# A fused attention and expert kernel: its hand-planned step list replaced by a second one

## The chip, the cores and the metric

The kernel runs on one core of one Trainium2 chip. Five engines work side by side, each through its own queue in order: PE (matrix products into PSUM), ACT (activations and copies), DVE (vector work and copies), POOL (masks, and the issue of the input loads) and SP (the issue of output stores and of crossbar transposes). The metric is device time of one execution in microseconds (us); lower is better. PSUM has eight banks, numbered 0 to 7.

## The reference

Two layers run one after the other over 8 batches of 576 tokens. The first is attention with 8 heads of 64, whose keys and values are averaged over 8 neighbouring tokens; the second is a causal attention in four experts, of which each token takes the best two. Cut to what matters:

```python
k_p = k.reshape(B, H, Sp, pool, D).mean(axis=3)      # pool = 8, Sp = 72
v_p = v.reshape(B, H, Sp, pool, D).mean(axis=3)
attn = softmax(scale * q @ k_p.T)                    # written out in the reference
x = (attn @ v_p) as [B, S, H * D]
logits = x @ w_gate; the best 2 of 4 experts, softmax over the two -> w
for e in range(4):
    a = softmax(causal(scale * (x @ wq[e]) @ (x @ wk[e]).T))
    out += w[e] * (a @ (x @ wv[e])) @ wo[e]
```

## The kernel before

The work of each batch is cut into small steps. A step belongs to one engine. The order of all steps on all engines is one text, `SEQ` (lines 622 to 694), which a planner's search wrote out; the loop behind it (line 696) reads it word by word and records each step's instructions, and each engine runs its own steps in that order. Waits between engines follow from which tile a step reads or writes. So the text alone decides what stands behind what on each engine, which PSUM bank a PE step writes, and on which of two engines a copy runs.

A word is name, arguments, a colon and the batch: `E1:4@26` is step E, argument 1, batch 4, in the banks from 2 and from 6 on. `@` gives the PSUM bank or banks of a PE step; a `d` at the end puts a copy on DVE, without it the copy runs on ACT; a `p` leaves the output store to a later word; a `c` runs a dummy matmul on 32 output rows only.

The steps in the order in which a batch passes through them:

- `L_k`, `L_q`, `L_v` (line 112): loads of the input, issued by POOL, which convert to bf16 on the way. `W` loads weights. For batch 0, `R` and `Q` load parts unconverted on other queues; `r` (line 140) and `w` (line 147) convert them, `c` orders weights.
- `PK`, `kc`, `kt` (lines 264 to 281): pool the keys on PE, transpose on DVE, copy to `kpT`. `PV`, `vc` (283, 286): the same for the values.
- `u` (line 292): DVE transposes q into `qT`. `u0` needs the pieces `L_q0` and `L_q2`, `u1` needs `L_q1` and `L_q3`.
- `E` (line 309): scores, in four banks; `e` (line 319): exp on ACT, each call over two banks. `E2` is the narrow one for the last 64 tokens.
- `D`, `d`, `x` (337 to 353): softmax denominators by PE, then logarithm and exp on ACT. `O`, `o` (356, 364): attention output on PE, scaled on DVE into `xT`.
- `V`, `v` (381, 391) and `P`, `p` (449, 457): projections of the experts, and their copies out of PSUM. `p_t` is the copy for the last 64 tokens. `g0` to `g9` (396): the gate.
- `S`, `s`, `a` (467, 480, 498): expert scores, exp on ACT, causal mask on POOL. Three of four `s` steps cover 128x1024.
- `B`, then `bz`, `bg`, `b` (526, 539): expert outputs on PE, and their scaling on DVE into `osc`.
- `osc` is transposed into `oT` on PE with a copy (`T`, `t`, lines 559 and 564) for batches 0, 1, 6 and 7, and by a crossbar DMA from SP's queue (`F`, line 574) for batches 2 to 5. `F10:5` moves the main part of expert pair 1 of batch 5, `F11:5` its tail.
- `Y`, `y`, `zs` (582, 592, 607): output projection on PE, copy to `ofin`, output store on SP's queue.
- `H` (line 205): dummy matmuls on a constant tile; nobody reads them.

Raw inputs have three buffers, so a load of batch b+3 waits for the steps that read batch b. PSUM banks have no fixed owner: a PE step that takes a bank waits for the bank's last reader.

Of the kernel before, what the change touches and what calls it, by code (L numbers as in the profile page):

```python
# [21 lines left out]
def kernel(  # L22
# [584 lines left out]
    def z(b, c, queue):  # L607
# [20 lines left out]
        d2:0 H1:0@1 H1:0@1 o10:0 x2:0 H1:0@1 H1:0@1 o20:0 H1:0@1 W3:0 H1:0@0 o11:0 H1:0@0 H1:0@0 c2:0d P_q0:0@2 L_v0:1
        c3:0d P_k0:0@3 L_v1:1 p_q0:0 P_t0:0@5 L_v2:1 p_k0:0 PK:1@2 p_t0:0 S00:0@0 L_k0:2 kc:1 S01:0@4 S02:0@6 s00:0
        P_q1:0@3 L_k1:2 kt:1d s02:0 L_k2:2 P_k1:0@2 u1:1 s01:0 a00:0 u0:1 a02:0 E1:1@06 p_k1:0 p_q1:0d L_q0:2 e11:1  # L630
        c4:0d L_q1:2 E0:1@24 e10:1 L_q2:2 V0:0@6 V1:0@7 e00:1 L_q3:2 v0:0d V2:0@0 v1:0d a01:0 V3:0@6 e01:1 v2:0d L_v0:2
        S12:0@2 v3:0d s12:0 g1:0 E2:1@04 L_v1:2 PV:1@6 g2:0 e21:1 g3:0 D0:1@7 e20:1 D1:1@2 a12:0 vc:1d H1:0@3 d0:1
# [10 lines left out]
        L_v2:4 g8:1 P_k0:2@3 g9:1 bz12:0 e00:3 bg12:0 L_k0:5 b12:0 PV:3@2 p_k0:2d L_k1:5 e01:3 E1:3@04 vc:3d B12:1@3
        L_k2:5 e10:3 P_k1:2@6 bz12:1 L_q0:5 bg12:1 b12:1 e11:3 T11:0@2 B02:0@7 p_k1:2d L_q1:5 V3:2@3 t11:0 bz02:0
        D0:3@0 a00:1 bg02:0 v3:2 O20:2@6 b02:0 D2:2@2 PK:4@1 d0:3 u0:4 L_q2:5 O00:3@3 O11:3@7 x0:3 a11:1 kc:4 D1:3@0
        T00:0@4 d2:2 V1:2@5 L_q3:5 d1:3 o00:3 T02:0@2 V0:2@1 x2:2 a10:1 t00:0d t02:0 Y3:0@0 x1:3 o20:2 L_v0:5 v0:2d
        S00:2@2 y3:0p O01:3@6 o11:3 D2:3@1 PV:4@4 s00:2 L_v1:5 zs3:0 o01:3 O10:3@0 B01:1@7 vc:4d d2:3 kt:4 Y1:0@6
# [5 lines left out]
        x0:4 S10:2@2 L_v1:6 p_t0:3d S12:2@6 O10:4@5 s10:2 p_k0:3d PV:5@0 a02:2 o10:4 O01:4@1 O00:4@4 vc:5 L_v2:6 D2:4@2
        V2:3@3 o01:4 d2:4 s12:2 B10:1@0 a10:2 o00:4 V3:3@2 B11:1@1 bz10:1 L_k0:7 v2:3 bg10:1 E2:5@46 v3:3 b10:1 V4:3@3
        bz11:1 e20:5 L_k1:7 bg11:1 b11:1 e21:5 V0:4@0 v4:3 g4:2 S03:2@4 L_k2:7 x2:4 S01:3@6 v0:4d S01:2@2 s03:2 T11:1@1
        g1:3 s01:3 T01:1@0 L_q0:7 T10:1@4 P_k0:4@5 t11:1d t10:1d t01:1d s01:2 g2:3 L_q1:7 Y3:1@4 g3:3 p_k0:4d E0:5@06
# [6 lines left out]
        B11:2@1 s12:3 p_k0:5d F00:2 a00:3 E0:6@26 bz11:2 bg11:2 P_q0:5@0 x2:5 b11:2 a12:3 e00:6 u1:6 F11:2 B00:3@1
        e01:6 p_q0:5d E1:6@24 bz00:3 F10:2 B11:3@0 bg00:3 b00:3 e10:6 V1:5@6 bz11:3 Y0:1@1 bg11:3 F01:3 e11:6 v1:5d
        B01:3@7 b11:3 Y2:1@6 y0:1p bz01:3 D0:6@0 bg01:3 b01:3 y2:1p PK:7@4 zs0:1 g1:4 O20:5@1 d0:6 D1:6@7 zs2:1 kc:7
        S12:4@2 F00:3 d1:6 P_k1:5@6 o20:5 s12:4 kt:7d g2:4 Y3:2@7 p_k1:5d x1:6 S03:4@0 S00:5@2 a12:4 S10:4@4 y3:2dp
        s03:4 V2:5@6 s00:5 a03:4 g3:4 V4:5@0 zs3:2 g4:4 v2:5d B10:3@7 s10:4 v4:5d a00:5 P_t0:5@6 bz10:3 E2:6@02 bg10:3
        x0:6 O01:6@4 a10:4 p_t0:5d e20:6 PV:7@5 b10:3 e21:6 O11:6@6 o01:6 O00:6@0 vc:7 F11:3 D2:6@7 O10:6@1 S01:4@2
# [107 lines left out]
```

## Time and profile before

| | us |
|---|---|
| median of 3 runs (156.7, 157.54, 157.59) | 157.54 |
| the profiled execution | 157.23 |
| its span, first to last instruction | 155.5 |
| busy: PE, ACT, DVE, POOL | 145.2, 137.8, 124.2, 89.0 |

The span is what the trace shows; 1.73 us of the execution's own time lie around it. Busy time is the time in which at least one instruction of the engine is under way; matmuls overlap, so PE's figure is no measure of how far PE is from its limit. PE's granted clock is 0.99 of full speed over the span. Line 220 is the helper of all matrix products, and line 211 that of all copies, so rows are told apart by the tiles they name. "From A to B" times count from the start of the span. In rows of single instructions the bracket at the end gives the engine's idle time ahead of it and what ended it.

### The profile page before, as it was taken

What the parts mean: (1) busy time and instruction counts of PE and PEld (TensorE: products, weight loads), DVE (VectorE), ACT (ScalarE), POOL (GpSimd) and SP (SyncE); (2) the same over time, 40 slices, a digit from 0 to 9 for tenths busy, and PEclk for the clock granted to TensorE, in tenths of its full rate; (3) what the DMA queues carried; (4) which work ended last, traced back from release to release, by engine and by line L of the source; (5) the groups of instructions that cost most, each with busy time, mean ns of one, the idle gap of its engine ahead of it and who ended that gap; (6) DMA issues with size and microseconds to landing.
All of it is one profiled execution on the core that took longest, in us unless ns stands there. A gap on an engine that the chain in (4) does not pass through costs nothing.

```text
span 155.5 us, 5467 instructions
## 1 busy us (share of the span) xinstructions
PE 145.2 (93%) x2131; PEld 79.1 (51%) x2131; DVE 124.2 (80%) x407; ACT 137.8 (89%) x255; POOL 89.0 (57%) x160
## 2 busy tenths in 40 slices
PE   6998998999999999999999999999999999969980
PEld 2332452454664365455736556475465765526640
DVE  1862826889889889989898999999988888957860
ACT  3369579999999999999999999999999999969970
POOL 6996488999689988855999141224100434323200
PEclk9999999999999999999999999999999999999997
DMA  4999999999999999999999963431480552387894
GB/s 121 239 187 184 177 179 180 180 180 190 180 179 180 182 177 181 213 251 178 180 180 213 181 75 76 146 104 34 126 279 8 108 173 72 82 198 267 282 377 161
DMA packets 68746, 26.67 MB, mean 171 GB/s; under 512 B 62704, under 2 KB 63728, under 8 KB 68720
## 3 DMA queue, kind: packets, MB, share of 16 engines
q0 software_dynamic: 57264, 14.72, 95.0%
q1 hardware_dynamic: 11088, 10.88, 22.8%
q10 hardware_dynamic: 368, 0.72, 1.5%
q8 instruction: 16, 0.26, 0.7%
q14 instruction: 10, 0.08, 0.2%
HBM read 30.42 MB, written 9.44 MB: 256 GB/s over the span
## 4 chain that ended last, share of the span: by engine, by line
PE 54%; DMA 19%; POOL 9%; ACT 7%; DVE 4%; issue 4%; POOLq 0%; SPq 0%; DVEq 0%; ACTq 0%
PE psum L220 53%; DMA qraw<-in_q_dram 11%; DMA wst_q<-in_moe_wq_dram 5%; DMA oT<-osc 3%; POOL kraw L125 3%; POOL qraw L125 3%; ACT eta L330 3%; ACT etb L493 2%; POOL vraw L125 1%; POOL etb L510 1%; PE psum L229 1%; DVE qT L297 1%; ACT rza L353 1%; ACT rza L349 1%; DVE osc L552 1%
## 5 line engine op out<-in xcount | busy, mean ns | idle before, releaser
L493 ACT ACTIVATE etb<-psum 128x1024 bf16<-128x1024 f32 x48 | 47.2, 1029 | 0.7 <-PE psum L220 0.4
L510 POOL TENSOR_SCALAR_AFFINE_SELECT etb<-etb 128x256 bf16<-128x256 bf16 x64 | 25.9, 416 | 30.0 <-ACT etb L493 29.1
L330 ACT ACTIVATE eta<-psum 96x1024 bf16<-96x1024 f32 (+1 forms) x48 | 36.0, 807 | 0.6 <-PE psum L220 0.2
L220 PEld LDWEIGHTS <-etb 128*128 128x128 bf16 x480 | 18.6, 97 | 7.9 <-issue 2.8
L376 DVE TENSOR_TENSOR xT<-psum,rza 128x512 bf16<-128x512 f32 x32 | 20.5, 681 | 2.1 <-ACT rza L353 2.0
L220 PE MATMUL psum<-wop,oT 128*128 128x512 bf16 (+1 forms) x74 | 20.4, 373 | 1.7 <-DMA oT<-osc 1.4
L125 POOL DMA_DIRECT2D qraw<-in_q_dram x29 | 19.1, 661 | 4.3 <-DMA vraw<-in_v_dram 2.9
L220 PE MATMUL psum<-vaug,etb 128*128 128x65 bf16 x480 | 21.2, 193 | 0.2 <-POOL etb L510 0.2
L125 POOL DMA_DIRECT2D kraw<-in_k_dram x25 | 19.0, 765 | 3.0 <-issue 0.9
L125 POOL DMA_DIRECT2D vraw<-in_v_dram x24 | 18.5, 774 | 3.7 <-PE psum L220 2.9
L220 PE MATMUL psum<-wvg,xT 128*128 128x260 bf16 x144 | 20.5, 274 | 0.0
L220 PE MATMUL psum<-xT,wqp 128*128 128x64 bf16 (+1 forms) x128 | 19.6, 286 | 0.0
L220 PE MATMUL psum<-xT,wkp 128*128 128x512 bf16 (+1 forms) x128 | 19.5, 286 | 0.0
L552 DVE TENSOR_TENSOR osc<-psum,gt 128x256 bf16<-128x256 f32 (+2 forms) x40 | 16.6, 422 | 1.0
L220 PE MATMUL psum<-qk 64*128 64x64 bf16 (+4 forms) x192 | 16.1, 277 | 0.2
L220 PEld LDWEIGHTS <-xT 128*128 128x128 bf16 x144 | 12.7, 97 | 6.3 <-issue 2.5
L211 ACT COPY ofin<-psum 128x512 f32<-128x512 f32 (+1 forms) x25 | 13.9, 581 | 2.1 <-PE psum L220 1.8
L211 DVE CAST qk<-psum 128x512 bf16<-128x512 f32 (+1 forms) x24 | 14.6, 615 | 1.3 <-PE psum L220 0.6
L297 DVE STREAM_TRANSPOSE qT<-qraw 128x576 f32<-128x576 f32 (+1 forms) x17 | 13.2, 789 | 2.9 <-DMA qraw<-in_q_dram 2.2
L220 PE MATMUL psum<-qT,kpT 32*128 32x64 bf16 (+1 forms) x256 | 13.3, 289 | 1.6 <-ACT eta L330 0.6
L208 PE MATMUL psum<-warm 128*128 128x512 bf16 x41 | 12.8, 461 | 1.3 <-DVE onesd L176 1.3
L220 PE MATMUL psum<-eta,vp 96*32 96x512 bf16 (+1 forms) x256 | 13.1, 288 | 0.2 <-DVE vp L211 0.2
(78 smaller groups left out, 215.8 us busy)
## 6 DMA issues: line engine op xcount, KB each, us to landing
out_dram<-ofin SPq DMA_DIRECT2D x32, 256.0 KB, 2.6
vraw<-in_v_dram POOLq DMA_DIRECT2D x24, 192.0 KB, 6.8
kraw<-in_k_dram POOLq DMA_DIRECT2D x21, 192.0 KB, 7.5
qraw<-in_q_dram POOLq DMA_DIRECT2D x28, 144.0 KB, 7.8
out_dram<-ofin SPq DMA_DIRECT2D x7, 128.0 KB, 2.5
xT<-in_q_dram ACTq DMA_DIRECT2D x2, 288.0 KB, 4.7
xT<-in_k_dram SPq DMA_DIRECT2D x2, 192.0 KB, 5.0
kraw<-in_k_dram POOLq DMA_DIRECT2D x4, 96.0 KB, 5.2
```

Of the source, the lines that this page charges most:

```text
L125: nc.gpsimd.dma_start(out=dst, in_=src)
L208: nc.tensor.matmul(out=psum[rows, bank, :], lhsT=warm[:, rows], rhs=warm[:], start=True, stop=True)
L211: (nc.vector.tensor_copy if dve else nc.scalar.copy)(out=out, in_=in_)
L220: nc.tensor.matmul(out=out, lhsT=lhsT, rhs=rhs, start=start, stop=stop)
L229: nc.tensor.transpose(out=out[s], in_=in_[:, s], identity=ident[0:n, 0:n])
L297: nc.vector.transpose(out=dst.rearrange("p (a s n) -> p a n s", s=32, n=n)[:, :, own], in_=src.rearrange("p (a n d) -> p a n d", n=n, d=32 ...
L330: nc.scalar.activation(out=dst, in_=src, func=EXP, scale=ATT_EXP_SCALE)
L349: nc.scalar.activation(out=rz, in_=z, func=LN)
L376: nc.vector.tensor_tensor(out=xT[:, 2 * got[0][0] + t : 2 * got[-1][0] + t + 1 : 2, m + got[0][1].start : m + got[0][1].stop], in0=psum[:, ...
L493: nc.scalar.activation(out=et[:, ep, :, eo : eo + n], in_=psum[:, bank : bank + 2, 0:n], func=EXP, scale=MOE_EXP_SCALE,)
L510: nc.gpsimd.affine_select(out=blk, in_=blk, pattern=[[0, 2], [1, 128]], compare_op=ISGE, fill=0.0, base=0, channel_multiplier=-1,)
L552: nc.vector.tensor_tensor(out=osc(b, ep)[:, own, :].rearrange("p c (e d) -> p e c d", e=2), in0=o[:, :, :, 0:HD], in1=gt.to_broadcast([128 ...
```

## The change

The text `SEQ` is replaced by another that holds the same steps of the computation, each with the same arguments. No function changes. There are three kinds of difference.

The order of the steps, almost everywhere behind the first line, and the banks of most PE steps. The loads keep their order among themselves.

The engine of some copies. Counted over the text, on ACT before and after (the rest runs on DVE):

| copy | on ACT before | on ACT after |
|---|---|---|
| `y` (to `ofin`, whole) | 24 | 18 |
| `p` (512 columns) | 14 | 15 |
| `p_t` | 2 | 4 |
| `vc` | 2 | 4 |
| `v` (two copies each) | 14 | 13 |
| `kt` | 6 | 4 |
| `t` (256 columns / 64 columns) | 3 / 3 | 4 / 5 |
| `r` | 1 | 0 |

The number of dummy matmuls: 41 before, 43 after, three of which use 32 output rows.

The diff at the places that the prediction speaks of:

```diff
-        R0:0 R1:0 Q0:0 Q1:0 I:0 H14:0@0 L_k20:0 L_k01:0 L_k11:0 J:0 K:0 M:0 L_k21:0 L_q1:0 w0:0 L_v0:0 r0:0d w1:0 u00:0
-        L_v1:0 r1:0 N:0 L_v2:0 PK0:0@0 H1:0@1 W0:0 H1:0@1 H1:0@1 u01:0 H1:0@1 W1:0 kc0:0 PK1:0@1 kt0:0 L_k0:1 kc1:0
...
-        v1:1 S12:1@6 s02:1 u0:3 S03:1@4 B11:0@3 a01:1 L_q2:4 u1:3 P_q0:2@2 s03:1 s12:1 bz11:0 a03:1 bg11:0 S11:1@0 g1:1
...
-        b02:1 e00:4 u1:4 P_q1:3@7 L_k1:6 y2:0dp e01:4 E1:4@02 L_k2:6 p_q1:3d V0:3@6 zs2:0 e10:4 L_q0:6 g1:2 T12:0@4
-        P_t0:2@7 v0:3d P_k1:3@5 L_q1:6 e11:4 t12:0d p_t0:2d g2:2 u1:5 V1:3@4 p_k1:3 L_q2:6 T02:1@2 E2:4@06 v1:3 D0:4@3
...
-        a12:2 y3:1p g4:3 V1:4@2 g5:2 u0:6 L_q2:7 e01:5 zs3:1 P_k1:4@3 v1:4d L_q3:7 g0:3 g6:2 e00:5 E1:5@46 g5:3 a01:2
...
-        F00:5 g2:7 Y0:2@7 s02:6 bz10:5 a10:6 B11:5@0 bg10:5 b10:5 P_k0:7@1 s11:6 bz11:5 a02:6 bg11:5 b11:5 F11:5
-        B00:6@6 y0:2dp Y3:4@2 p_k0:7 a11:6 Y1:4@0 bz00:6 y3:4p zs0:2 bg00:6 F10:5 B11:6@1 b00:6 y1:4p S02:7@4 zs3:4
-        bz11:6 S01:7@2 g0:7 bg11:6 S00:7@6 zs1:4 s02:7 b11:6 P_q1:7@0 g3:7 g4:7 g5:7 s00:7 g6:7 B10:6@1 a02:7 T00:6@4
-        P_k1:7@5 bz10:6 bg10:6 p_q1:7 t00:6d a00:7 b10:6 s01:7 T11:6@4 Y1:5@6 p_k1:7d Y3:5@7 t11:6d y1:5p S03:6@0 a01:7
...
+        R0:0 R1:0 Q0:0 Q1:0 I:0 H14:0@0 L_k20:0 L_k01:0 L_k11:0 J:0 K:0 M:0 L_k21:0 L_q1:0 w0:0 L_v0:0 r0:0d w1:0 r1:0d
+        L_v1:0 u01:0 L_v2:0 u00:0 PK0:0@0 H1:0@1 W0:0 H1:0@1 kc0:0 H1:0@1 H1:0@1 kt0:0d W1:0 N:0 PK1:0@0 E0:0@24 L_k0:1
...
+        E2:0@02 E1:0@46 e21:0 H1:0@4c e20:0 H1:0@4c L_q1:1 e11:0 H1:0@4c e10:0 PV:0@0 L_q2:1 D0:0@1 D2:0@6 vc:0d d0:0
...
+        V4:1@1 V1:1@6 p_q1:1d L_q1:4 v4:1 T10:0@0 S03:1@2 u0:3 v1:1 a01:1 S11:1@4 s03:1 L_q2:4 S02:1@6 u1:3 s11:1
...
+        e00:4 t02:0d t00:0d P_k0:3@1 v1:3d L_k1:6 e01:4 g1:2 E2:4@26 B12:1@0 p_k0:3d L_k2:6 e21:4 S02:2@4 e20:4 bz12:1
+        T01:1@1 bg12:1 E1:4@26 s02:2 b12:1 t01:1d g2:2 B10:1@0 L_q0:6 g3:2 V0:3@1 e11:4 bz10:1 B02:1@4 bg10:1 L_q1:6
+        v0:3d P_k1:3@5 e10:4 bz02:1 bg02:1 a02:2 b10:1 B11:1@1 b02:1 p_k1:3 u1:5 T12:1@0 L_q2:6 S10:2@6 t12:1 S11:2@2
...
+        E2:5@02 g6:2 T11:1@4 L_k2:7 p_t0:3d Y1:0@5 e21:5 t11:1d e20:5 S03:2@6 S01:2@2 L_q0:7 y1:0dp S12:2@0 s03:2
...
+        e11:5 u1:6 P_k0:4@5 a01:2 y3:1dp e10:5 L_q3:7 E0:5@26 p_k0:4d zs3:1 L_v0:7 PV:5@4 e00:5 g2:3 D2:4@5 V1:4@0 g3:3
...
+        bz11:5 a00:6 bg11:5 b11:5 B10:6@7 bg10:5 S00:7@0 p_q1:7 b10:5 a12:6 S02:6@2 V0:7@4 s00:7 bz10:6 F11:5 bg10:6
+        b10:6 Y2:4@6 v0:7d s02:6 Y0:4@5 a00:7 y2:4dp Y3:4@7 F10:5 S02:7@0 y0:4p zs2:4 a02:6 y3:4dp S01:7@2 V1:7@6 s02:7
+        zs0:4 zs3:4 B00:6@7 P_k1:7@5 v1:7d s01:7 a02:7 g1:7 Y0:3@6 bz00:6 bg00:6 g0:7 p_k1:7 b00:6 Y1:4@4 a01:7 g2:7
+        y0:3p Y1:3@2 g3:7 g4:7 S12:7@0 y1:4p zs0:3 g5:7 S03:6@6 y1:3dp T00:6@5 s12:7 T10:6@3 zs1:4 Y3:5@4 t00:6d zs1:3
...
```

More of the change, by code (lines that the diff above doesn't have):

```diff
@@ L628 @@
[L628 to L632, printed above, removed]
@@ L643 @@
[L643 to L647, printed above, removed]
@@ L653 @@
[L653 to L656, printed above, removed]
-        a12:2 y3:1p g4:3 V1:4@2 g5:2 u0:6 L_q2:7 e01:5 zs3:1 P_k1:4@3 v1:4d L_q3:7 g0:3 g6:2 e00:5 E1:5@46 g5:3 a01:2
@@ L663 @@
[L663 to L667, printed above, removed]
```

98 lines of the change are left out of this document (57 added, 41 removed).

## The prediction

> **What bounds the kernel now.** I read the page first, then the engines' busy time by stretch, then the waits of the transposes that follow the loads, then the tail. The page's head, and its picture of the DMA engines in 40 slices:
>
> ```profile
> span 155.5 us, 5467 instructions
> PE 145.2 (93%) x2131; PEld 79.1 (51%) x2131; DVE 124.2 (80%) x407; ACT 137.8 (89%) x255; POOL 89.0 (57%) x160
> DMA  4999999999999999999999963431480552387894
> ```
>
> PE shows most, but a matmul's record overlaps the next one (a dummy's row further down shows it), so 93% isn't PE at its limit. The DMA engines are full from the second slice to about slice 22, some 86 us: that is the stream of q, k and v. By stretch (columns: length, then busy time and count of PE, PEld, DVE, ACT, POOL, then clock, DMA share, GB/s):
>
> ```profile
> 47.00:136.00 89.00, 88.42 (x1390) 50.76 (x1389) 81.50 (x270) 87.75 (x166) 46.97 (x91) 1.00 1.06 148
> 136.00:140.00 4.00, 2.58 (x21) 0.97 (x20) 2.20 (x6) 2.71 (x7) 0.95 (x3) 1.00 0.82 198
> ```
>
> From 47 to 136 us ACT works 87.75 of 89.00 us: there ACT is the bound, and DVE has 7.50 us of idle time. Before 47 us something else sets the pace. The DVE rows of the q transposes (start, length, engine, and in brackets what DVE waited for) say what:
>
> ```profile
> 23.85 1.44 DVE L297 STREAM_TRANSPOSE qT<-qraw 128x576 f32<-128x576 f32 x2 [0.93 <-DMA qraw<-in_q_dram]
> 35.32 1.44 DVE L297 STREAM_TRANSPOSE qT<-qraw 128x576 f32<-128x576 f32 x2 [0.18 <-DMA qraw<-in_q_dram]
> 46.46 1.44 DVE L297 STREAM_TRANSPOSE qT<-qraw 128x576 f32<-128x576 f32 x2 [0.36 <-DMA qraw<-in_q_dram]
> 66.91 0.78 DVE L297 STREAM_TRANSPOSE qT<-qraw 128x576 f32<-128x576 f32 x1 [0.47 <-DMA qraw<-in_q_dram]
> ```
>
> By their order in the list these are batches 1, 2, 3 and 5, some 11 us apart from batch to batch, each started when its q had just landed. POOL's loads stand in the same order in both lists and the DMA engines are full, so these landings stay where they are. Work taken from an engine ahead of such a row buys waiting at that row and no time at the end. I therefore take the start of `u0:3` at 46.46 as a clock, and count only what changes behind it. The last piece is the tail (PE, then ACT, then SP's queue, then the chain that ended last):
>
> ```profile
> 138.48 0.82 PE L220 MATMUL psum<-wop,oT 128*128 128x512 bf16 x3 [1.42 <-DMA oT<-osc]
> 138.91 0.59 ACT L211 COPY ofin<-psum 128x512 f32<-128x512 f32 x1 [1.29 <-PE psum L220]
> 134.62 0.53 SPq L615 DMA_DIRECT2D out_dram<-ofin  x1
> 135.21 1.25 SPq L580 DMA_TRANSPOSE oT<-osc  x1
> 135.21 3.23 DMA oT<-osc
> ```
>
> Crossbar step `F10:5` was issued at 135.21, right behind the output store `zs0:2` (134.62), and landed 3.23 us later. PE stood 1.42 us at `Y1:5` for it, ACT 1.29 us behind PE.
>
> **The change part by part.** The sum is made against the profiled execution, 157.23 us (span 155.5 and 1.73 around it); it lies 0.31 below the median of 157.54, within the three runs.
>
> *Copies that change engine.* ACT's prices, by form:
>
> ```profile
> L211 ACT COPY ofin<-psum 128x512 f32<-128x512 f32 x24 | 13.6, 589 | 1.6 <-PE psum L220 1.3
> L211 ACT CAST qk<-psum 128x512 bf16<-128x512 f32 x14 | 8.3, 590 | 2.9 <-PE psum L220 2.9
> L211 ACT CAST qk<-psum 128x256 bf16<-128x256 f32 x2 | 0.8, 382 | 0.0
> L211 ACT CAST vp<-psum 96x512 bf16<-96x512 f32 x2 | 1.2, 582 | 0.0
> L211 ACT CAST vaug<-psum 128x256 bf16<-128x256 f32 x14 | 5.2, 383 | 0.0
> L211 ACT COPY L<-psum 128x4 f32<-128x4 f32 x14 | 2.5, 182 | 0.0
> L211 ACT COPY oT<-psum 128x64 bf16<-128x64 bf16 x3 | 0.6, 229 | 0.0
> L211 ACT COPY oT<-psum 128x256 bf16<-128x256 bf16 x3 | 1.1, 371 | 0.4 <-PE psum L229 0.4
> L211 ACT CAST kpT<-kf 128x192 bf16<-128x192 f32 x2 | 0.7, 352 | 1.2 <-DVE kf L277 1.2
> L211 ACT CAST kpT<-kf 128x384 bf16<-128x384 f32 x4 | 2.1, 519 | 0.0
> L211 ACT CAST qraw<-xT 128x576 bf16<-128x576 f32 x1 | 0.7, 667 | 0.0
> ```
>
> Over the whole list ACT loses six `y` (3.53 us), one `v` (0.383 + 0.182 = 0.57), two `kt` (0.352 + 0.519 = 0.87) and `r1` (0.67), and gains one `p` (0.59), two `p_t` (0.76), two `vc` (1.16), two small `t` (0.46) and a large one (0.37): 5.64 - 3.34 = 2.30 us less. Behind `u0:3` the count is another: six `y` less (3.53) and two `v` less (1.13), but two `p` (1.18), three `p_t` (1.15), two `vc` (1.16), two small `t` (0.46) and one large (0.37) more: **0.34 us less**. The other 1.96 us lie ahead of the clock, where I cost them at nothing; the load stream hides them, and without that cover they'd count in full (first rival).
>
> DVE's side behind `u0:3`, at most:
>
> ```profile
> L211 DVE COPY ofin<-psum 128x512 f32<-128x512 f32 x11 | 7.5, 683 | 2.2 <-issue 1.7 <-PE psum L220 0.3
> L211 DVE CAST vaug<-psum 128x256 bf16<-128x256 f32 x22 | 9.2, 420 | 1.6 <-PE psum L220 0.9 <-ACT etb L493 0.3
> ```
>
> Six `y` are 4.10 us and three `v` 1.26, together 5.36, before what DVE hands back in `p`, `vc` and `t`. That fits into the 7.50 us idle shown above: nothing on the path.
>
> *The crossbar of batch 5.* Between the last `b` step that `F10:5` reads and the first `Y` of batch 5, the old list has 12 PE steps and, on ACT, three `s`, two `p` and two `y`; the new one has 17 PE steps and five `s`, one `p` and three `y`. An `s` is priced here:
>
> ```profile
> L493 ACT ACTIVATE etb<-psum 128x1024 bf16<-128x1024 f32 x48 | 47.2, 1029 | 0.7 <-PE psum L220 0.4
> ```
>
> That makes 2 x 1.03 + 0.59 - 0.59 = 2.06 us more distance. On SP's queue `F10:5` now follows `F11:5` directly, and `zs0:2` is four words ahead. 2.06 covers the 1.42 us wait, with 0.64 to spare. ACT being the bound, I take off its share, **1.29 us**; the bounds are 0.65 (half stays) and 1.42. Next late there is the last chain `B12:7`, `b12`, `T12`, `t12`, `Y4:7`, which both lists end with.
>
> *Banks taken over whole.* `E1:4@26` now follows `E2:4@26` on the same four banks, and `S12:2@0` takes the pair that `e20:5` reads last; before, these E steps shared two banks, read earlier. PE's wait of this sort, and the read it can wait for:
>
> ```profile
> 12.16 0.63 PE L220 MATMUL psum<-qT,kpT 32*128 32x512 bf16 x8 [0.39 <-ACT eta L330]
> L330 ACT ACTIVATE eta<-psum 96x256 bf16<-96x256 f32 x16 | 5.3, 385 | 0.0
> ```
>
> Each costs between nothing (other PE and ACT steps in between) and two reads, 0.77. I take the wait shown, 0.39 each: **+0.78 us**; range 0 to 1.54. Behind the waiting matmul PE's whole queue stands, and ACT's next `s` and `e` wait for that.
>
> *Two more dummy matmuls* (43 for 41), some in other places:
>
> ```profile
> 16.28 2.55 PE L208 MATMUL psum<-warm 128*128 128x512 bf16 x11
> ```
>
> 2.55 / 11 = 0.23 us each (their records overlap), so 0.46 for two. They stand ahead of rows 23.85 and 35.32, in PE's waits for q: nothing; 0.46 if that cover is gone, and no gain either, as PE's clock reads 1.00 throughout.
>
> *Gate steps, masks, transposes and stores* are the same in number; they change places only. A part I can't price from before is the packing of some 1,100 steps between 47 and 136 us. ACT's idle time there is 1.25 us now; this may vanish or grow several times over. The range and the last rival carry it.
>
> Sum: 157.23 - 0.34 - 1.29 + 0.78 = 156.38, so **156.4 us**. By its own bounds: 157.23 - 0.34 - 1.42 = 155.5 to 157.23 - 0.34 - 0.65 + 1.54 = 157.8.
>
> **The rivals.**
>
> First, the ACT relief counts in full: if ACT ran through from start to end, 157.23 - 2.30 - 1.29 = **153.6**, without bank waits. For it: 98.6% of ACT's time after 47 us. Against: four rows in which q's landing ended the wait.
>
> Second, the crossbar wait is only moved: SP's queue or the last transposes hold PE as long elsewhere. 157.23 - 0.34 + 0.78 = **157.7**. For it: the last 16 us are full of hand-overs, and PE's steps there fall behind each other.
>
> [...]
>
> Fourth, slower: batch 6's q is now wanted at once. `u1:6` moves forward, ahead of `u0:6`; the old list had `u0:6` here:
>
> ```profile
> 79.59 0.77 DVE L297 STREAM_TRANSPOSE qT<-qraw 128x576 f32<-128x576 f32 x1
> L125 POOL DMA_DIRECT2D qraw<-in_q_dram x1: 662/662/662, 70.7 to 70.7; - x1
> DMA to landing us min/median/max: 7.7/7.7/7.7
> POOL etb L510 <- ACT etb L493: 29.1, 24, 6.2
> ```
>
> The last q load of batch 6 is issued at 70.7 and lands at 78.4, 1.2 us before 79.59. In the new list mask `a02:2` stands on POOL between `L_q1:6` and `L_q2:6`, and a mask waits for its exp, up to 6.2 us (last row). If this load comes x us later, DVE stops x - 1.2 us at `u1:6`, and with it everything behind in order. At x = 6.2: 156.4 + 5.0 = **161.4**; it decides for slower from x = 4.0 (159.2). For it: exp steps of batch 2 run late wherever PE waits for a bank. Against: eight loads are under way at a time, which hides a short delay.
>
> **How the numbers follow.** One per cent around 157.54, about what this kernel's measurement tells from no change, is 155.96 to 159.12. Chances: the forecast 0.39, of which 0.11 fall below 155.96 (its range begins at 155.5, and ACT's 1.25 us idle may also shrink) and 0.01 above 159.12; first rival 0.18; second 0.14; third 0.03; fourth 0.26. Faster: 0.18 + 0.11 = 0.29. Slower: 0.26 + 0.01 = 0.27. The same: 0.44. The range: 154.0 leaves out about half of the first rival (0.09), 160.2 some 0.4 of the fourth (0.11); between them lies 0.8. The forecast's own range is 155.5 to 157.8.
>
> **What would show it.** Right: the transposes of batches 1 to 3 again start near 23.9, 35.3 and 46.5 us behind a wait for q, longer than 0.18 and 0.36, since ACT and DVE come there earlier; ACT's busy time falls by about 2.3 us while the span falls by about 1; no PE wait for `oT` over 0.4 us in the last 20 us; a PE wait of some 0.4 us at `E1:4`. Wrong: the q transposes start earlier than now (the clock isn't the loads, first rival); the 1.3 us turn up elsewhere on PE in the tail (second); loads land over 1 us later from the start (third); a DVE wait for q of batch 6 near 80 us (fourth); or ACT's idle time between 47 and 136 us grows well over 1.25 us in many small waits, which would be none of these.

## The result, and the profile after

The changed kernel takes 157.79 us (median of 20 runs, 157.11 to 158.96), the kernel before 157.18 us beside it (20 runs): a ratio of 1.0045, 95% interval 1.0028 to 1.0062. A second set gives 157.67 us and 1.0024 (1.0007 to 1.0041). So it is a little slower, by 0.2 to 0.5%, where 0.7% faster was forecast.

The profiled execution took 158.05 us. The page's head, which counts some matmuls less because their records are missing:

```profile
span 156.3 us, 5432 instructions
PE 142.4 (91%) x2106; PEld 79.2 (51%) x2133; DVE 127.2 (81%) x410; ACT 135.9 (87%) x252; POOL 89.0 (57%) x160
```

ACT works 1.9 us less than before (137.8), and the span is 0.8 us longer. Cut at 47 us, behind the transposes that the prediction took for a clock, the span can be added up from ACT's side: 47 us, its busy time behind them, and its idle time behind them. Busy time by stretch (columns as in the prediction: length, then PE, PEld, DVE, ACT, POOL), first the kernel before, from 47 us to its end and then in parts:

```profile
47.00:155.50 108.50, 101.86 (x1556) 58.49 (x1554) 92.77 (x315) 100.70 (x192) 50.37 (x99) 0.99 1.01 167
...
76.00:90.00 14.00, 13.85 (x224) 7.70 (x222) 13.01 (x46) 13.63 (x29) 10.14 (x19) 1.00 1.77 189
...
102.00:120.00 18.00, 18.00 (x279) 10.05 (x275) 16.71 (x53) 17.75 (x34) 3.00 (x8) 1.00 0.37 112
...
136.00:148.00 12.00, 10.58 (x134) 6.11 (x133) 8.86 (x35) 10.40 (x20) 3.39 (x9) 1.00 0.80 250
```

The same of the changed kernel:

```profile
47.00:156.30 109.30, 100.45 (x1545) 58.91 (x1562) 94.64 (x317) 99.53 (x187) 50.23 (x99) 1.00 1.00 166
...
76.00:90.00 14.00, 12.85 (x225) 7.39 (x227) 13.46 (x39) 12.68 (x23) 7.50 (x14) 1.00 1.69 207
...
102.00:120.00 18.00, 16.43 (x239) 8.56 (x238) 15.09 (x48) 15.77 (x28) 2.46 (x6) 1.00 0.41 104
...
136.00:148.00 12.00, 11.71 (x165) 7.53 (x168) 10.72 (x46) 11.79 (x24) 4.31 (x11) 1.00 0.80 276
```

ACT's work behind 47 us falls by 100.70 - 99.53 = 1.17 us, its idle time there grows from 7.80 to 9.77, by 1.97; together +0.8, the change of the span. By stretch the idle time changes by -1.39 from 136 to 148 us (1.60 to 0.21, the old crossbar wait), **+1.98 from 102 to 120** (0.25 to 2.23), **+0.95 from 76 to 90** (0.37 to 1.32), and +0.43 in all the rest together. The gain that was forecast is there, and it is given back earlier in the span. The two largest new waits of this profile, by the instructions that end them (start, length, in brackets the idle time ahead of it and what ended it):

```profile
79.53 1.02 PE L220 MATMUL psum<-xT,wkp 128*128 128x512 bf16 x4 [0.99 <-DVE qk L211]
81.15 1.02 ACT L330 ACTIVATE eta<-psum 96x1024 bf16<-96x1024 f32 x1 [1.16 <-PE psum L220]
107.39 1.47 PE L220 MATMUL psum<-wop,oT 128*128 128x512 bf16 x5 [1.36 <-DMA oT<-osc]
108.03 1.07 ACT L211 COPY ofin<-psum 128x512 f32<-128x512 f32 x2 [1.57 <-remote]
```

By their place in the list the first is `P_k0:4@5`, which needs bank 5 from the copy `p_k1:4d`; DVE comes to that copy late, behind the gate steps `g9:2` and `g1:3`. The other is `Y4:3`, the output projection of the last 64 tokens of batches 2 and 3, which needs the crossbar's tail piece `F01:3`. "remote" at ACT's `y4:3` stands for the same wait, passed on by PE. That piece was issued at 102.9 us and flew for 4.5 us:

```profile
L577 SPq DMA_TRANSPOSE oT<-osc x1: 1179/1179/1179, 102.9 to 102.9; - x1
DMA to landing us min/median/max: 4.5/4.5/4.5
```

### The profile page after: what moved, and what is told of

The parts are those of the page before. It is cut to its first block, busy times and chain, and to the rows that moved or that the text cites. A ratio compares the mean times of both kernels' runs of the same rounds, so it can differ in the third digit from the quotient of the medians.

```text
span 156.3 us, 5432 instructions
## 1 busy us (share of the span) xinstructions
PE 142.4 (91%) x2106; PEld 79.2 (51%) x2133; DVE 127.2 (81%) x410; ACT 135.9 (87%) x252; POOL 89.0 (57%) x160
## 5 line engine op out<-in xcount | busy, mean ns | idle before, releaser
L493 ACT ACTIVATE etb<-psum 128x1024 bf16<-128x1024 f32 x48 | 46.4, 1025 | 1.1 <-PE psum L220 0.3
L220 PE MATMUL psum<-xT,wkp 128*128 128x64 bf16 (+1 forms) x122 | 18.5, 282 | 1.9 <-DVE qk L211 1.0
L220 PE MATMUL psum<-vaug,etb 128*128 128x65 bf16 x480 | 20.1, 193 | 0.1
L220 PE MATMUL psum<-wop,oT 128*128 128x512 bf16 (+1 forms) x64 | 18.0, 373 | 2.0 <-DMA oT<-osc 1.4
L220 PE MATMUL psum<-xT,wqp 128*128 128x64 bf16 (+1 forms) x120 | 18.8, 280 | 0.6
L220 PE MATMUL psum<-qk 64*128 64x448 bf16 (+4 forms) x192 | 15.9, 277 | 0.8 <-DVE xT L376 0.4
L211 DVE CAST qk<-psum 128x512 bf16<-128x512 f32 (+1 forms) x21 | 13.3, 633 | 1.8 <-PE psum L220 1.2
L208 PE MATMUL psum<-warm 128*128 128x512 bf16 (+1 forms) x40 | 12.4, 456 | 1.7 <-DVE onesd L176 1.3
L211 DVE COPY ofin<-psum 128x512 f32<-128x512 f32 (+1 forms) x18 | 11.9, 669 | 2.0 <-PE psum L220 1.9
L211 ACT COPY ofin<-psum 128x512 f32<-128x512 f32 (+1 forms) x19 | 10.7, 581 | 2.7 <-remote 1.6
```

Of the source, the lines that this page charges most:

```text
L208: nc.tensor.matmul(out=psum[rows, bank, :], lhsT=warm[:, rows], rhs=warm[:], start=True, stop=True)
L211: (nc.vector.tensor_copy if dve else nc.scalar.copy)(out=out, in_=in_)
L220: nc.tensor.matmul(out=out, lhsT=lhsT, rhs=rhs, start=start, stop=stop)
L493: nc.scalar.activation(out=et[:, ep, :, eo : eo + n], in_=psum[:, bank : bank + 2, 0:n], func=EXP, scale=MOE_EXP_SCALE,)
```

## The experiments

Ratios are to the kernel before, run beside each kernel on the same chip, with 95% intervals. The diffs show the words around an edit; the lines of the list go on at both ends.

### Do the two waits come again, and does taking them away pay?

**The changed kernel unedited.**

> The changed kernel once more, unedited, as the yardstick of the next three. Theory: its two stalls belong to its order and come again: PE waits 0.9 to 1.5 us for the tail crossbar F01:3 at Y4:3 near 107 us, and about 1 us near 80 us for bank 5, whose reader stands on DVE behind two gate steps that last 0.7 us and more; ratio to before 1.002 to 1.007. Rival: one or both were chance of the one profiled execution; then that row has under 0.3 us here, and the ratio still stands at 1.0045, so that the loss lies elsewhere.

Measured: 157.67 us, 1.0024 (1.0007 to 1.0041). The row of `Y4:3`:

```profile
106.58 1.47 PE L220 MATMUL psum<-wop,oT 128*128 128x512 bf16 x5 [0.92 <-DMA oT<-osc]
```

and the two stretches:

```profile
76.00:90.00 14.00, 13.64 (x238) 7.76 (x234) 13.04 (x41) 13.54 (x26) 7.57 (x14) 1.00 1.69 207
...
102.00:120.00 18.00, 16.87 (x251) 9.15 (x254) 15.58 (x48) 16.27 (x28) 2.48 (x6) 1.00 0.38 98
```

The crossbar wait recurs. The wait near 80 us does not (ACT's idle time in its stretch is 0.46, not 1.32), but a smaller one of another kind stands further on, at `PK:7`, which needs the keys of batch 7. Here, and in the run of the next edit:

```profile
85.43 0.29 PE L220 MATMUL psum<-kraw,poolk 96*32 96x128 bf16 x8 [0.20 <-DMA kraw<-in_k_dram]
```

```profile
85.25 0.29 PE L220 MATMUL psum<-kraw,poolk 96*32 96x128 bf16 x8 [0.64 <-DMA kraw<-in_k_dram]
```

The new list puts `PK:7` at 85.5 us, the old one at 97.6; its last load lands at 85.4 us in the profile of this run and in the first profile of the kernel before. So the loads set PE's pace once more, well behind `u0:3`. The execution of this profile took 157.24 us, 0.8 less than the first.

**`Y4:3` some 3 us further back.**

```diff
-        V4:5@5 vc:7 o10:6 x0:6 Y4:3@4 F10:3 v4:5d Y3:2@1 y4:3p o01:6 Y1:1@6 y3:2p S00:5@2
-        o00:6 zs4:3 S10:4@4 S11:4@0 zs3:2 s00:5 y1:1dp P_k1:5@7
+        V4:5@5 vc:7 o10:6 x0:6 F10:3 v4:5d Y3:2@1 o01:6 Y1:1@6 y3:2p S00:5@2 S11:4@0
+        o00:6 zs3:2 s00:5 y1:1dp Y4:3@4 s11:4 y4:3p zs4:3 S10:4@4 P_k1:5@7
...
-        a00:5 P_k1:6@6 p_k1:5d s11:4
+        a00:5 P_k1:6@6 p_k1:5d
```

> The changed kernel with the tail projection Y4:3 some 3 us further back, behind Y3:2, Y1:1, S00:5 and S11:4. Theory: the wait for the crossbar F01:3 at 107 us lies on the path, since ACT has work all the time behind it; taking it away shortens the execution by 1.2 to 1.5 us, ratio to before 0.994 to 0.998. Rival: the wait is made up for further on, where ACT catches up, or the crossbar lands later still; then the gain is under 0.4 us, ratio 1.002 to 1.007.

Measured: 158.89 us, 1.0112 (1.0073 to 1.0152), slower by over 1 us. The crossbar wait is gone, and behind it stands a new one:

```profile
109.34 0.45 PE L220 MATMUL psum<-qk 64*128 64x512 bf16 x2 [1.67 <-ACT ofin L211]
```

`S10:4@4` takes the bank of `Y4:3@4` right behind it and so waits for `y4:3`, which stands behind `s11:4` on ACT. The edit made this wait; the run says nothing on the price of the old one.

**The gate steps behind the copy that frees bank 5.**

```diff
-        s01:2 g9:2 g1:3 E1:5@06 a12:2 p_k1:4d
+        s01:2 E1:5@06 a12:2 p_k1:4d g9:2 g1:3
```

> The changed kernel with the gate steps g9:2 and g1:3 behind the copy p_k1:4 on DVE, so that bank 5 comes free before them. Theory: PE's wait of 0.99 us and ACT's of 1.16 us near 80 us go, and with them 0.8 to 1.1 us of the execution, ratio to before 0.997 to 1.000. Rival: the next hand-over takes the wait's place (E1:5 on banks 0 and 6, or the gate's own readers later), gain under 0.3 us, ratio 1.003 to 1.006. Second rival: the gate steps are long wherever they stand, and hold the next DVE copies up: gain 0.3 to 0.6.

Measured: 157.53 us, 1.0018 (1.0002 to 1.0034). No gain beside the unedited 1.0024, as is to be expected where the wait seldom stands: ACT's idle time from 76 to 90 us is 0.50 with the edit and 0.46 without.

**Both edits.**

> Both edits of the two runs before together. Theory: the two waits lie one behind the other on ACT's path and add up: 2.0 to 2.5 us less than the changed kernel, about 155.4 us, ratio to before 0.988 to 0.992, so faster than both kernels. Rival: something behind 110 us sets the end (the load of ACT's last steps, the crossbars of batch 5), so the two together give no more than the larger one, 1.2 to 1.5 us, ratio 0.995 to 0.997.

Measured: 158.45 us, 1.0100 (1.0063 to 1.0137): the bank wait of the first edit again, 1.72 us.

### What was the old crossbar wait worth, and is there a clock?

**The kernel before, its wait for `F10:5` mended twice over.**

```diff
-        y3:4p zs0:2 bg00:6 F10:5 B11:6@1
+        y3:4p bg00:6 F10:5 zs0:2 B11:6@1
...
-        T11:6@4 Y1:5@6 p_k1:7d Y3:5@7 t11:6d y1:5p S03:6@0 a01:7
-        S10:7@2 y3:5dp S11:7@4 s03:6 zs1:5
+        T11:6@4 p_k1:7d t11:6d S03:6@0 a01:7
+        S10:7@2 s03:6 Y1:5@6 Y3:5@7 y1:5p S11:7@4 y3:5dp zs1:5
```

> The kernel before with its own crossbar wait mended by hand: F10:5 ahead of the store zs0:2 on SP, and Y1:5 and Y3:5 two exp steps (S03:6, S10:7) further back. Theory: the 1.42 us of PE and 1.29 us of ACT at Y1:5 were on the path, as the prediction took them to be; the kernel before becomes 0.8 to 1.3 us faster, ratio 0.992 to 0.995. Rival: the wait was hidden by what comes behind it (the transposes and crossbars of the last batches end no earlier), gain under 0.3 us, ratio 0.998 to 1.001; then the prediction's term of 1.29 us was wrong in the changed kernel too.

Measured: 157.00 us, 0.9996 (0.9980 to 1.0012): nothing. Again a new wait, here on ACT at the projection's copy, which now comes too late to fill the place it had filled:

```profile
138.42 0.58 ACT L211 COPY ofin<-psum 128x512 f32<-128x512 f32 x1 [0.72 <-PE psum L220]
```

ACT's idle time from 136 to 148 us is 1.60 us, as much as in the kernel before.

**Four copies ahead of `u0:3` back on ACT.** By the prediction's rows they are 0.58 + 0.59 + 0.52 + 0.58 = 2.27 us (the expectations put `kt` at 0.87 and so say up to 2.6).

```diff
-vc:1d  p_k0:1d  kt:2d  vc:2d
+vc:1   p_k0:1   kt:2   vc:2
```

> The changed kernel with four copies ahead of u0:3 (vc:1, p_k0:1, kt:2, vc:2) put from DVE back on ACT: about 0.58 + 0.59 + 0.87 + 0.58 = 2.6 us more work for ACT ahead of 46 us. Theory (the clock): the q loads set the pace there, and the execution grows by 0 to 0.4 us, ratio to before 1.004 to 1.007. Rival (ACT counts in full): 2.0 to 2.6 us more, ratio 1.017 to 1.021. Between the two: the clock covers a part, namely the waits that stand ahead of the q rows.

Measured: 156.90 us, 0.9993 (0.9978 to 1.0008): faster than the changed kernel by 0.5 to 0.8 us with more work on ACT. That work is less than 2.27 us: ACT's busy time is 137.09 us, 1.20 more than in the first profile of the changed kernel and 0.89 more than in the second (136.20), because the records of neighbouring ACT instructions overlap (in the kernel before the lengths of ACT's 255 records add up to 158.8 us, while ACT is busy for 137.8). Its profile has no wait for a crossbar at all: `F01:3` flew 2.3 us. PE's wait at `PK:7` is not there either, as PE comes to it after the landing (ACT's idle time from 76 to 90 us is 0.30). That makes the run no clean test of the clock.

**Four copies behind `u0:3` back on ACT**, `kt:5`, `p_k0:4`, `vc:5`, `p_q0:5`, edited in the same way.

> The counterpart: four copies behind u0:3 (kt:5, p_k0:4, vc:5, p_q0:5) put from DVE back on ACT, again about 0.87 + 0.59 + 0.58 + 0.59 = 2.6 us more work for ACT, now between 66 and 90 us. Theory: ACT is the bound there, and the execution grows by 1.8 to 2.6 us, ratio to before 1.016 to 1.021. Rival (ACT isn't the bound there either, PE and DVE hand-overs are): under 0.8 us, ratio under 1.010.

Measured: 158.84 us, 1.0121 (1.0087 to 1.0156), 1.2 us more than the unedited 157.67, or 1.5 us by the ratios. That lies between the two expectations, but ACT's busy time rises by 1.24 us only (136.20 to 137.44), not by the copies' 2.28, so the copies count in full. The wait at `Y4:3` is there too (1.68 us on PE); from 76 to 90 us ACT's idle time is down to 0.20, so part of the new work went into waits.

**Without the three dummies on 32 rows** (`H1:0@4c`).

> The changed kernel without its three dummy matmuls on 32 rows. Theory: they stand in PE's waits and PE's granted clock doesn't need them: no change, ratio to before 1.003 to 1.006, clock 0.99 as now. Rival: without them the clock falls somewhere ahead of 47 us, which shows as a granted clock below 1.00 in that stretch and, where PE isn't covered by a wait, up to 0.5 us more.

Measured: 157.52 us, 1.0038 (1.0012 to 1.0065). No change; the dummies cost nothing and bring nothing that shows: from 0 to 47 us the granted clock reads 1.00 without them as with them.

### What holds the crossbar, and the price of its places

Sixteen crossbar steps of the first profiles, set beside the DMA engines' other packets, pointed at one thing: instruction fetches (the packets on the two queues that the DMA view calls `instruction`: q8, 16 KB a packet, and q14, 8 KB). The slice of the changed kernel from 104.4 to 107.4 us has one of each, starting at 104.5 (8 KB) and 105.2 us:

```profile
q8 instruction: 1, 0.02, 2.6%
q14 instruction: 1, 0.01, 1.1%
```

**Fetches moved.** 80 matmuls of 64 columns stand in for 8 of the 14 dummies that open PE's list, to make the 16 KB fetches that follow come earlier.

```diff
-        I:0 H14:0@0 L_k20:0
+        I:0 H6:0@0 h80:0@0 L_k20:0
...
+    def tiny(n, bank):
+        for _ in range(n):
+            nc.tensor.matmul(out=psum[:, bank, 0:64], lhsT=warm[:, 0:128], rhs=warm[:, 0:64], start=True, stop=True)
```

> The changed kernel with 80 small dummy matmuls (64 columns) in place of 8 of the 14 large ones that open PE's list, so that every later fetch of PE's instructions, 16 KB each, comes some 80 matmuls earlier; nothing else moves. Theory: a crossbar transpose doesn't move data while an instruction fetch is under way, and lands 0.85 to 1.05 us behind the fetch's end; the fetch that held F01:3 (105.2 us) now comes near 102, F01:3 flies 2.2 to 3.2 us instead of 4.0 to 4.7, PE's wait at Y4:3 falls under 0.3 us and the execution gets 0.8 to 1.3 us shorter, ratio to before 0.995 to 1.000. Rival: fetches and long flights fall together by chance; then F01:3 still flies 4 us and more, and the ratio stays at 1.002 to 1.005.

Measured: 157.40 us, 1.0027 (1.0006 to 1.0048). The flight of `F01:3` (line 577 is 581 here, 220 is 224), and PE at `Y4:3`:

```profile
L581 SPq DMA_TRANSPOSE oT<-osc x1: 1180/1180/1180, 104.6 to 104.6; - x1
DMA to landing us min/median/max: 2.4/2.4/2.4
```

```profile
107.07 1.25 PE L224 MATMUL psum<-wop,oT 128*128 128x512 bf16 x5
```

From the trace's records, flights in us and the starts of the fetches:

| | changed kernel | fetches moved |
|---|---|---|
| 16 KB fetches | 98.0, 105.2, 118.6, 123.6, 131.9, 143.6 | 94.2, 103.2, 112.4, 119.7, 128.7, 137.2 |
| `F01:3`, issued 102.9 / 104.6 | 4.46 | 2.44 |
| `F01:4`, issued 122.0 / 121.7 | 3.98 | 2.30 |
| `F10:4`, issued 128.4 / 127.8 | 2.57 | 4.31 |
| `F10:5`, issued 135.5 / 135.2 | 2.50 | 4.06 |

The long flights went where the fetches went. `F01:3` was itself issued 1.7 us later; the other three, issued within 0.6 us of their old times, are the cleaner comparison. The time did not follow: idle time of ACT from 102 to 120 us fell from 1.73 to 1.00, but from 76 to 90 it was 1.14 in this execution, 0.58 us of PE's wait at `PK:7` among it.

**`Y4:3` back again, in bank 7** (6 and 7 change names from there on).

```diff
-        x0:6 Y4:3@4 F10:3 v4:5d Y3:2@1 y4:3p o01:6 Y1:1@6 y3:2p S00:5@2
-        o00:6 zs4:3 S10:4@4 S11:4@0 zs3:2 s00:5 y1:1dp P_k1:5@7 g1:5 zs1:1 s10:4 g2:5 a00:5 P_k1:6@6
+        x0:6 F10:3 v4:5d Y3:2@1 o01:6 Y1:1@6 y3:2p S00:5@2
+        o00:6 S10:4@4 zs3:2 Y4:3@7 S11:4@0 s00:5 y1:1dp P_k1:5@6 g1:5 zs1:1 s10:4 y4:3p zs4:3 g2:5 a00:5 P_k1:6@7
```

> The changed kernel with Y4:3 behind Y3:2, Y1:1, S00:5 and S10:4 again, but in bank 7 (banks 6 and 7 change names from there on), so that S10:4 does not wait for y4:3, as it did for 1.7 us in the first try. Theory: PE's wait at 107 us was on the path; the execution gets 0.8 to 1.3 us shorter than the changed kernel, ratio to before 0.995 to 0.999. Rival: the last 20 us set the end whatever comes ahead of them, gain under 0.3 us, ratio 1.001 to 1.005.

Measured: 157.31 us, 1.0014 (0.9994 to 1.0034). No wait at `Y4:3`, but `P_k1:6`, now in bank 7, waits for `y4:3` and holds `E0:7` behind it, and ACT stands at `e00:7`:

```profile
111.07 1.93 ACT L330 ACTIVATE eta<-psum 96x1024 bf16<-96x1024 f32 x2 [0.74 <-PE psum L220]
```

**The kernel before, with SP's order alone changed**: the first of the two edits above, `F10:5` ahead of the store `zs0:2`.

> The kernel before with nothing changed but SP's order: F10:5 ahead of the store zs0:2, some 0.6 us earlier; the projections stay where they are. Theory (the prediction's step 2): PE's 1.4 us wait at Y1:5 falls to 0.3 or less and the execution gets 0.8 to 1.3 us shorter, ratio 0.992 to 0.995. Rival (from the run that moved the projections too): the wait goes, but the transposes of the last batch end as late as ever, ratio 0.998 to 1.001. Second rival: no wait of that size in most executions of the kernel before, so nothing to gain.

Measured: **155.64 us, 0.9910 (0.9891 to 0.9929)**, 1.6 us by the medians and 1.4 by the ratio faster than the kernel before, and the fastest of all. `F10:5` is issued at 134.0 us, 1.2 earlier than in the first profile of the kernel before (135.2), and flies 2.5 us instead of 3.2:

```profile
L580 SPq DMA_TRANSPOSE oT<-osc x1: 1222/1222/1222, 134.0 to 134.0; - x1
...
DMA to landing us min/median/max: 2.5/2.5/2.5
```

Of the 2.0 us by which it lands earlier, 1.3 come from the issue and 0.8 from the shorter flight: an 8 KB fetch that lay inside the flight (136.5 us) now begins (136.2) just ahead of the landing. PE has no wait for it left, and ACT's idle time behind 47 us falls from 7.80 to 106.60 - 100.37 = 6.23:

```profile
47.00:153.60 106.60, 101.50 (x1556) 58.88 (x1554) 92.84 (x314) 100.37 (x192) 49.83 (x99) 0.99 1.03 170
```

**The kernel before once more.**

> The kernel before once more, for a second profile. Theory: its wait for F10:5 near 137 us belongs to its order and comes again with 1.0 to 1.6 us. Rival: chance of one execution, under 0.5 us here.

Measured: 157.65 us. The wait belongs to the order:

```profile
138.56 0.82 PE L220 MATMUL psum<-wop,oT 128*128 128x512 bf16 x3 [1.59 <-DMA oT<-osc]
```

**The third try with `Y4:3`**, with `E0:7` ahead of `P_k1:6`.

```diff
-        a00:5 P_k1:6@7 p_k1:5d s11:4
-        E0:7@24 g4:4
+        a00:5 p_k1:5d s11:4
+        E0:7@24 P_k1:6@7 g4:4
```

> The second try with Y4:3, and E0:7 moved ahead of P_k1:6, which had waited for y4:3 in bank 7 and held E0:7 for 0.6 us. Theory: both waits between 102 and 112 us are then gone, ACT runs through from 102 to 114 us with under 0.4 us idle (2.23 us over 102 to 120 in the first profile of the changed kernel), and the execution falls to 156.3 to 156.9 us, ratio to before 0.994 to 0.998. Rival: PE's work, not one wait, sets the pace there, and ACT waits as long one step later; ratio 1.000 to 1.003 as in the second try.

Measured: 157.32 us, 1.0020 (1.0004 to 1.0035): the rival. The wait moved on by one step once more, to `E1:7` and its exp, because `P_q0:6` now waits in bank 7 for `p_k1:6`:

```profile
113.33 1.93 ACT L330 ACTIVATE eta<-psum 96x1024 bf16<-96x1024 f32 x2 [1.10 <-PE psum L220]
```

**The same, with the four copies ahead of `u0:3` back on ACT.**

> The kernel of the run before, and the four copies ahead of u0:3 put back on ACT (vc:1, p_k0:1, kt:2, vc:2, 2.3 to 2.6 us more for ACT). With the crossbar wait out of both, this is the clean test of the prediction's clock. Theory (the clock): 0 to 0.4 us more than the run before. Rival (ACT counts in full): 2.0 to 2.6 us more. Second rival: fewer and slower hand-overs on DVE were what helped the first time, then 0.3 us or more less.

Measured: 158.11 us without one execution of 160.10, 1.0063 (1.0035 to 1.0092): 0.7 us more than the run before by the ratios, 0.8 by the medians: between clock and full. ACT has the same 1.10 us wait in both. By the profiles ACT's busy time is 1.20 us more (135.97 to 137.17), 0.99 of it behind 47 us (99.59 to 100.58), so the q loads covered little of it. But from 76 to 90 us ACT's idle time falls from 0.73 to 0.30, since PE no longer comes to `PK:7` ahead of its load (it waited 0.56 us there in the run before).

**The wait put in by itself.** The kernel with four copies back on ACT has no wait at `Y4:3`. Here SP issues `F00:3` first and `F01:3` second; no bank and no other order changes.

```diff
-        g3:4 F01:3 v0:5d
+        g3:4 F00:3 v0:5d
...
-        o20:5 F00:3 zs2:2
+        o20:5 F01:3 zs2:2
```

> The kernel with four copies back on ACT ahead of u0:3, which has no crossbar wait at Y4:3, and one edit on SP's queue alone: F00:3 and F01:3 change places, so that the later of the two, which an instruction fetch near 105 us holds, is now the one that Y4:3 needs. No bank, copy or other order changes. Theory: F01:3 lands near 108 to 109 us, PE waits 2 to 3 us at Y4:3, and since this place is on the path the execution grows by 1.5 to 2.8 us, ratio to before 1.009 to 1.017. Rival: work behind it catches up (ACT has waits of its own further on), under 0.8 us more, ratio under 1.005.

**Its yardstick.**

> The kernel with four copies back on ACT ahead of u0:3 once more, unedited, beside the run with the swap. Theory: that it has no wait at Y4:3 belongs to where its instruction fetches fall, and comes again: F01:3 flies 2.2 to 2.5 us, ratio to before 0.997 to 1.001. Rival: chance of one call; then F01:3 flies 4 us here, and the ratio is 1.002 and more.

Measured: 158.85 us, 1.0108 (1.0064 to 1.0152) with the swap, 157.12 us, 0.9998 (0.9978 to 1.0018) without: **1.73 us more**. With the swap, `F01:3` is issued 0.6 us later and flies 3.46 us instead of 2.29 (in both profiles without the swap, the 8 KB fetch that comes at 104.5 us in the changed kernel comes at 106.1 and 107.0, behind the landing), and

```profile
107.76 1.47 PE L220 MATMUL psum<-wop,oT 128*128 128x512 bf16 x5 [1.63 <-DMA oT<-osc]
...
108.40 1.07 ACT L211 COPY ofin<-psum 128x512 f32<-128x512 f32 x2 [1.84 <-remote]
```

PE's wait of 1.63 and ACT's of 1.84 us cost 1.73 us: the place is on the path, one for one. ACT's idle time from 102 to 120 us is 2.50 with the swap:

```profile
102.00:120.00 18.00, 16.16 (x236) 8.37 (x237) 14.79 (x49) 15.50 (x28) 2.47 (x6) 1.00 0.35 105
```

and 0.69 without:

```profile
102.00:120.00 18.00, 17.79 (x275) 9.92 (x276) 16.50 (x53) 17.31 (x32) 2.47 (x6) 1.00 0.47 116
```

## Why the prediction was wrong

The time of 157.79 us is inside the range, and the case "within 1%" came; the sign of the forecast and its sum are wrong. That they are not further off is partly luck: the +0.78 for banks did not come, and without it the sum would have been 155.6. Step by step:

**The clock: half right.** The transposes stand where the prediction put them, `u0:3` at 46.59 for 46.46, and it waits longer, 0.80 for 0.36; batch 6's transpose does not wait, so the slower rival (its load late) fell:

```profile
23.18 1.44 DVE L297 STREAM_TRANSPOSE qT<-qraw 128x576 f32<-128x576 f32 x2 [0.83 <-DMA qraw<-in_q_dram]
34.94 1.43 DVE L297 STREAM_TRANSPOSE qT<-qraw 128x576 f32<-128x576 f32 x2
46.59 1.44 DVE L297 STREAM_TRANSPOSE qT<-qraw 128x576 f32<-128x576 f32 x2 [0.80 <-DMA qraw<-in_q_dram]
79.40 0.76 DVE L297 STREAM_TRANSPOSE qT<-qraw 128x576 f32<-128x576 f32 x1
```

But that a transpose keeps its time doesn't mean that work ahead of it counts nothing: ACT ran other work forward past it. Its work behind 47 us is 1.17 us less in the first profile and 0.50 in the second (100.70 to 100.20), where 0.34 was counted; the transpose at 34.94 no longer waits at all; and the 1.20 us that four copies ahead of the clock add to ACT's busy time cost 0.7 to 0.8 in the pair without the wait at `Y4:3`. So of the 1.96 us that were costed at nothing, between 0.2 and 0.8 came through as less work of ACT behind 47 us. The first rival (in full) fell. Four copies behind the clock cost 1.2 to 1.5 us for 1.24 us of busy time: the difference between the two sides is smaller than the prediction made it. The prices themselves were too high: the mean length of an ACT record includes its overlap with the next one, which the prediction noted for PE alone, and the relief of 2.30 us over the whole list measured 1.9 and 1.6. Nor is `u0:3` the last place where a load sets the pace: `PK:7` is another, and the prediction did not look at the loads of the keys.

**The crossbar wait of batch 5: right, in size too.** -1.29 was counted; moving `F10:5` ahead of one store, and nothing else, brought 1.4 us by the ratio (0.7 to 1.1%, or 1.1 to 1.7 us), and in the changed kernel ACT's idle time there is 1.39 less. The second rival (only moved elsewhere in the tail) fell.

**Banks taken over whole: wrong, 0 for +0.78.** PE has no idle time on record from 73 to 77 us, where `S12:2@0` stands, and comes to `E1:4@26` without any:

```profile
64.95 0.63 PE L220 MATMUL psum<-qT,kpT 32*128 32x512 bf16 x8
```

**Dummies: right.** Three of them taken out changed nothing. **Loads landing over 1 us later, the sign named for the third rival: not there.** The first row above is 0.67 us earlier than before, and POOL's issues of q, k and v loads take 659, 765 and 775 ns each, for 661, 765 and 774; no run shows a cast on DVE holding them up. **DVE's copies: not tested by themselves.** The wait at 79.53 us ended with a copy on DVE, but `p_k1:4` runs there in both lists; it was late because two gate steps took 1.10 and 0.75 us.

**The step that failed is the one that left "the packing of some 1,100 steps between 47 and 136 us" out of the sum.** That part was not small change: ACT's idle time from 47 to 136 us went from 1.25 to 4.50 us, and most of it stands in few places. The prediction counted the distance from the last `b` step to the first reader for one crossbar, the one that waited before. It should have been counted for all sixteen, tail pieces included, and likewise from the loads to their readers where the list moves a reader forward by 12 us, as it does `PK:7`. For `F01:3` in the changed kernel the distance is short: PE came to `Y4:3` at 107.39 - 1.36 = 106.03, 3.1 us behind the issue at 102.89 (read from the profile after; ahead of the run it would have had to be counted in steps, as for `F10:5`). By the typical flight of tail pieces in the kernel before, that is enough; by its longest it isn't:

```profile
L577 SPq DMA_TRANSPOSE oT<-osc x8: 1103/1174/1727, 90.9 to 133.4; - x8
DMA to landing us min/median/max: 2.3/2.4/4.1
```

4.1 - 3.1 = 1.0 us is the price that this gives, as an upper end. The flight was 4.46 and 4.01 us, and PE's wait 1.36 and 0.92 us, nearly all of it on the path by what the swap shows. What is left of ACT's idle time between 102 and 120 us without that wait, 0.69 for 0.25, is small hand-overs, 0.28 or 0.29 us of them at `e20:7` in the profiles of the new order.

With the measured terms the first profile adds up as 157.23 - 1.17 (ACT's work behind 47 us) - 1.39 (old crossbar) + 1.98 (102 to 120 us) + 0.95 (76 to 90 us) + 0.43 (the rest) = 158.03, for 158.05. Of the +0.95 only a part is the order's. In seven profiles with this stretch of the new list as it stands, ACT's idle time from 76 to 90 us is 0.46 to 1.32, 0.78 on average; in four of the old list it is 0.31 to 0.43. So the new list loses some 0.4 us there. The wait for bank 5 is 0.99 us in the first profile and 0.17 in one other; the wait at `PK:7` stands in the other six, 0.20 to 0.64 us, and no run priced it by itself.

That the crossbar wait is the whole loss isn't shown: three runs had it taken out of the changed kernel and won back 0.3 to 0.4 us beside 157.67 by the medians and next to nothing beside 1.0024 by the ratios, no more than the intervals. Two of them have a bank wait of their own behind it; in the third, with the fetches moved, ACT stood 1.14 us from 76 to 90 in its profile, and whether it does so each time is open. What is shown is that the wait is on the path, 1.73 us for 1.63 where one swap on SP's queue puts it in, and that the one variant which misses it is 0.5 to 0.8 us faster in spite of 0.9 to 1.2 us more busy time on ACT; that variant misses the wait at `PK:7` too.

## What to carry to other kernels

Where a transfer feeds a step in a planned order, count the distance from its issue to its first reader for every such transfer, and set it against the longest flight in the profile, not the median; a wait that stands once in the old order can stand elsewhere in the new one, and a step moved forward can come to stand ahead of its load's landing. Before a plan is searched anew, try the one move that the wait names: one store moved behind one crossbar step was worth 1.4 us, more than the whole new order. A step moved away from a wait takes its bank and its filler with it, so a failed edit by hand is no evidence that the wait was free; putting the wait in, with nothing else changed, prices it.

## What the runs showed of the hardware

**A crossbar transpose lands late where an instruction fetch falls into its flight.** Over 18 profiles, 288 crossbar steps: the 99 that have no fetch of 8 or 16 KB inside their normal length (about 2.25 us for a tail, 2.48 for a main piece) all land in 2.20 to 2.66 us. 136 take over 0.5 us longer, up to 4.87, and each of them has such a fetch; they land 1.2 us (median; 0.85 to 2.29 in the first profiles of the two kernels) behind the end of the last fetch in their flight. 53 have a fetch and are not long: what decides is where in the flight it falls. Of 111 steps with a fetch under way between 1.4 and 2.1 us behind the issue, 110 are long; of the other 177, 26. That the fetch is the cause is shown by moving it: the long flights moved along, from `F01:4` (3.98 to 2.30 us) to `F10:4` and `F10:5` (2.57 to 4.31 and 2.50 to 4.06). How it holds the crossbar is not shown, nor whether data stand still meanwhile, as the expectation of that run had it; whether an engine waited for a fetch was not examined here.

**Small DVE operations run long beside masks on POOL.** In the first profile, DVE's `g9:2` and `g1:3`:

```profile
77.02 1.10 DVE L444 TENSOR_TENSOR G<-W,rden 128x16 f32<-128x16 f32 x1
78.05 0.75 DVE L414 TENSOR_TENSOR hi<-L 128x10 f32<-128x10 f32 x1
```

and POOL's rows at that time, two load issues and the masks:

```profile
76.31 1.31 POOL L125 DMA_DIRECT2D qraw<-in_q_dram  x2
77.62 0.43 POOL L502 TENSOR_SCALAR_AFFINE_SELECT etb<-etb 64x256 bf16<-64x256 bf16 x1
77.99 0.77 POOL L510 TENSOR_SCALAR_AFFINE_SELECT etb<-etb 128x256 bf16<-128x256 bf16 x2
```

Each operation ends when a mask ends (78.1 and 78.8). The first began 0.60 us ahead of the first mask, during a load issue, so the mask alone doesn't account for its 1.10 us. In the second profile the same two start before the masks:

```profile
77.50 0.17 DVE L444 TENSOR_TENSOR G<-W,rden 128x16 f32<-128x16 f32 x1
77.58 0.16 DVE L414 TENSOR_TENSOR hi<-L 128x10 f32<-128x10 f32 x1
```

```profile
77.65 0.46 POOL L502 TENSOR_SCALAR_AFFINE_SELECT etb<-etb 64x256 bf16<-64x256 bf16 x1
```

Over the 18 profiles these two lines of the gate have 432 operations, of which 360 take at most 0.2 us. Of the 72 longer ones 69 began while a mask was under way, and 68 end 0.01 to 0.11 us behind the end of a mask. Of the 360, 98 began during a mask too, all but 2 of them in its first 0.02 or its last 0.10 us.

So the second row, 0.75 us where the second profile has 0.16, ran 0.59 us longer beside a mask, and the count says the same of most long ones. That the mask is the cause is not shown: no run moved one by itself.

**Behind a long wait PE's clock fell in two profiles, and not in three others.** In the profile of the kernel without the three dummies (159.41 us, where the median is 157.52) PE waits 1.76 us at `Y4:3`, up to 107.20 us. From 107 to 111 us its granted clock then reads 0.54, 0.50, 0.50 and 0.75 by windows of 1 us, and six matmuls take 2.74 us. Over the stretch (the last three columns are clock, DMA share and GB/s):

```profile
102.00:120.00 18.00, 16.24 (x228) 7.68 (x226) 13.32 (x45) 14.06 (x23) 2.24 (x6) 0.91 0.39 93
```

ACT is idle for 3.94 us there. The first try with `Y4:3` shows the same, 0.91 over the stretch, behind its wait of 1.67 us. But behind waits of 1.63, 1.68 and 1.72 us (the swap, the four copies behind `u0:3`, both edits) the clock stays at 1.00, so the length of the wait alone does not decide. The executions with a lower clock are long ones: of the 20 of the changed kernel, three have a mean clock of 0.987 to 0.988 and take 158.46 to 158.96 us, the other 17 have 0.991 and more and a median of 157.62. Where the fall stands in these three is not shown.
